# Splitting the later filter loads over two DMA queues, and releasing the weight loads after the last filter group

## The chip, the cores and the metric

The kernel runs on one core of a Trainium2 chip. The metric is the time of one execution on the device, in microseconds (us). Executions are in a fast or a slow state. In the slow state the granted TensorE clock is low (0.655 in one profile below), and such runs are set aside. A "profile" is one traced execution. Times inside a profile count from its first instruction, and its span is 1.5 to 2 us shorter than the time of the execution.

Each DMA is issued by an engine's queue: SyncE (SP), ScalarE (ACT) or GpSimd (POOL). A transfer has "landed" when its completion semaphore, the counter that others wait for, has got its last count. To "evict" is to copy TensorE's results to where the next step reads them.

## The reference, cut to what matters

```python
X = np.fft.rfft(x, axis=1)                     # x: 8 batches x 3008 x 256
y = np.fft.irfft(X * (filt_r + 1j*filt_i), n=3008, axis=1)
h = y.reshape(24064, 256) @ w_in               # 256 -> 2048
out = (h / (1 + exp(-beta*h))) @ w_out         # 2048 -> 256
```

The kernel does the Fourier transforms as small matmuls. Batch 0 is transformed in a set-up of some 38 us. The main loop then multiplies by the weights, and the transforms of the later batches are worked in between its steps.

## The kernel before

In the set-up the filter comes in three groups of columns. GpSimd issues the first, SyncE the other two. Each group is four transfers: a lower and an upper half, of the real and of the imaginary filter. SyncE issues a tiny transfer (`mark`) first. It reads the third piece of the first x, so SyncE's queue is held until that piece has landed.

```python
mark = dpool.tile([1, D], BF16, name="mark", tag="mark")
nc.sync.dma_start(mark[:], x_cur[:1, JG, :])
...
FG = ((0, KG), (KG, KG), (2 * KG, 2 * KG))
for h in range(2):
    for f, at in ((filt_r, 0), (filt_i, M)):
        load_filter(fri, f, at, *FG[0], gp)[h]()
for h in (1, 0):
    for f, at in ((filt_r, 0), (filt_i, M)):
        load_filter(fri, f, at, *FG[1], nc.sync)[h]()
for h in (0, 1):
    for f, at in ((filt_r, 0), (filt_i, M)):
        load_filter(fri, f, at, *FG[2], nc.sync)[h]()
```

VectorE multiplies with the filter: 12 steps of two products. Steps 0 to 2 need the first group, 3 to 5 the second, 6 to 11 the third.

```python
for dst, ps in zip((p_t, q_t), pss):
    nc.vector.tensor_tensor(dst[:], ps[:], fri[:, 2 * i : 2 * i + 2, :], ALU.mult)
```

GpSimd issues the weights and the second x, after a tiny copy (`held`) that waits for filter rows:

```python
for p0 in (H, M + H):
    gp.tensor_copy(held[p0 : p0 + H], fri[p0 : p0 + H, 2 * KG - 1, :1])
load_win(0); load_win(1); load_wout(0)
xs[1] = load_x(1, X_HALVES[:2])
...                                  # at step 3 of the products:
load_wout(1)
load_x(1, X_HALVES[2:], xs[1])
mark3 = dpool.tile([1, D], BF16, name="mark3", tag="mark3")
nc.sync.dma_start(mark3[:], xs[1][:1, J - 1, :])   # holds SyncE's queue until this x is there
load_wout(2); load_wout(3)
...
for at in (0, M):                                  # four loads, next on SyncE's queue
    for go in load_filter(frr, filt_r, at, 0, JG, nc.sync): go()
```

## Time and profile before

| | before |
|---|---|
| time, five fast runs | median 792.15 us (790.61 to 792.77) |
| span of the profile | 788.4 us |
| TensorE busy | 777.5 us (99%) |
| first matmul of the main loop | 38.26 us |

The engine line of the page of the kernel before says what bounds it: TensorE is busy nearly all the time.

```profile
span 788.4 us, 15540 instructions
PE 777.5 (99%) x6111; PEld 547.9 (69%) x6111; DVE 394.4 (50%) x647; ACT 597.4 (76%) x920; POOL 144.6 (18%) x143
```

The next lines are from the timeline of VectorE, kernel before: start, duration, instruction, and in brackets the idle time before it and what the profile takes for the releaser. They are the products of steps 0, 3 and 6, the first users of the three filter groups.

```profile
17.18 0.69 DVE L446 TENSOR_TENSOR pb_t<-ps,fri 128x512 bf16<-128x512 f32 x1 [1.23 <-PE ps L437]
...
21.24 0.68 DVE L446 TENSOR_TENSOR pb_t<-ps,fri 128x512 bf16<-128x512 f32 x1
...
27.01 0.69 DVE L446 TENSOR_TENSOR pb_t<-ps,fri 128x512 bf16<-128x512 f32 x1 [0.64 <-PE ps L437]
```

```profile
51.53 0.59 PE L825 MATMUL hps<-y,win_sb 128*128 128x512 bf16 x2
51.96 0.33 PE L546 MATMUL ps<-t4b,zz 96*128 96x94 bf16 x4
```

### The profile page before, as it was taken

What the parts mean: (1) busy time and instruction counts of PE and PEld (TensorE: products, weight loads), DVE (VectorE), ACT (ScalarE), POOL (GpSimd) and SP (SyncE); (2) the same over time, 40 slices, a digit from 0 to 9 for tenths busy, and PEclk for the clock granted to TensorE, in tenths of its full rate; (3) what the DMA queues carried; (4) which work ended last, traced back from release to release, by engine and by line L of the source; (5) the groups of instructions that cost most, each with busy time, mean ns of one, the idle gap of its engine ahead of it and who ended that gap; (6) DMA issues with size and microseconds to landing.
All of it is one profiled execution on the core that took longest, in us unless ns stands there. A gap on an engine that the chain in (4) does not pass through costs nothing.

```text
span 788.4 us, 15540 instructions
## 1 busy us (share of the span) xinstructions
PE 777.5 (99%) x6111; PEld 547.9 (69%) x6111; DVE 394.4 (50%) x647; ACT 597.4 (76%) x920; POOL 144.6 (18%) x143
## 2 busy tenths in 40 slices
PE   8899999999999999999999999999999999999997
PEld 5766667766777667876668766686667766776665
DVE  7847835646536564465635746267462761500101
ACT  6887886886678866788677876778767788677776
POOL 9422500420014200131002310024000340000000
PEclk9999999999999999999999999999999999999999
DMA  9978687116901187012860238412370214100101
GB/s 193 233 199 214 161 207 206 48 67 187 234 27 67 48 214 206 28 67 94 198 176 27 95 103 186 151 55 85 103 215 29 74 67 127 51 31 28 54 27 54
DMA packets 84057, 91.46 MB, mean 116 GB/s; under 512 B 4434, under 2 KB 74212, under 8 KB 82962
## 3 DMA queue, kind: packets, MB, share of 16 engines
q1 hardware_dynamic: 80880, 73.95, 30.6%
q0 software_dynamic: 2816, 16.26, 10.6%
q8 instruction: 48, 0.79, 0.4%
q10 hardware_dynamic: 288, 0.26, 0.1%
q14 instruction: 25, 0.20, 0.1%
HBM read 57.16 MB, written 46.66 MB: 132 GB/s over the span
## 4 chain that ended last, share of the span: by engine, by line
PE 90%; DMA 5%; DVE 3%; issue 1%; POOL 0%; DVEq 0%; ACT 0%; POOLq 0%; SPq 0%; ACTq 0%
PE acc L860 40%; PE hps L825 39%; PE ps L621 3%; PE ps L546 2%; PE ps L643 2%; PE ps L669 2%; DMA fri<-in_filt_i_dram 1%; DMA d<-a 1%; DVE ost L109 1%; DMA xg<-in_x_dram 1%; DMA mark<-xg 1%; DMA a<-d 0%; DVE qb_t L446 0%; DVE q_t L658 0%; DVE pb_t L446 0%
## 5 line engine op out<-in xcount | busy, mean ns | idle before, releaser
L834 ACT ACTIVATE gT<-hps,beta_sb 128x512 bf16<-128x512 f32 x752 | 516.8, 687 | 175.2 <-PE hps L825 165.5
L860 PE MATMUL acc<-wout_sb,gT 128*128 128x256 bf16 x3008 | 455.1, 272 | 1.2 <-ACT ost L107 0.2
L825 PE MATMUL hps<-y,win_sb 128*128 128x512 bf16 (+8 forms) x1730 | 447.7, 351 | 0.0
L860 PEld LDWEIGHTS <-gT 128*128 128x128 bf16 x3008 | 285.4, 98 | 132.4 <-issue 4.3
L825 PEld LDWEIGHTS <-win_sb 128*128 128x128 bf16 x1730 | 164.9, 98 | 24.3 <-issue 0.2
L659 POOL TENSOR_TENSOR v_t<-p_t,q_t 128x512 bf16<-128x512 f32 x84 | 106.7, 1271 | 374.5 <-DVE q_t L658 371.6
L109 DVE COPY ost<-acc 128x512 f32<-128x512 f32 (+1 forms) x88 | 56.2, 677 | 193.6 <-PE acc L860 190.6
L109 DVE CAST a<-ps 96x512 bf16<-96x512 f32 x96 | 65.8, 686 | 86.1 <-PE ps L621 83.7
L111 DVE TENSOR_SCALAR y<-ps 128x376 bf16<-128x376 f32 (+1 forms) x119 | 64.4, 545 | 63.1 <-PE ps L546 62.9
L654 DVE TENSOR_TENSOR p_t<-ps,frr 128x512 f32<-128x512 f32 x84 | 58.1, 692 | 32.4 <-PE ps L643 29.8
L658 DVE TENSOR_TENSOR q_t<-ps,fri 64x512 f32<-64x512 f32 x84 | 58.3, 694 | 1.2
L655 DVE SCALAR_TENSOR_TENSOR q_t<-ps,fri 64x512 f32<-64x512 f32 x84 | 57.5, 684 | 1.1
L546 PEld LDWEIGHTS <-zz 96*128 96x128 bf16 x512 | 35.3, 97 | 28.9
L107 ACT ACTIVATE z<-ps 128x512 bf16<-128x512 f32 x84 | 49.5, 590 | 0.8 <-PE ps L669 0.7
L621 PE MATMUL ps<-xg,t 94*96 94x512 bf16 x112 | 41.9, 381 | 0.0
L546 PE MATMUL ps<-t,zz 96*128 96x94 bf16 x448 | 36.7, 204 | 0.0
L118 POOL DMA_DIRECT2D xg<-in_x_dram x22 | 12.1, 557 | 114.3 <-PE acc L860 97.7
L669 PE MATMUL ps<-v_t,t 128*128 128x256 bf16 x168 | 32.1, 273 | 0.6 <-DVE q_t L658 0.6
L643 PE MATMUL ps<-a,t 128*128 128x256 bf16 x168 | 32.1, 273 | 0.3 <-DMA a<-d 0.3
L643 PEld LDWEIGHTS <-t 128*128 128x128 bf16 x168 | 15.9, 98 | 15.0 <-issue 0.4
L621 PEld LDWEIGHTS <-t 94*96 94x96 bf16 x112 | 13.8, 123 | 12.1
L669 PEld LDWEIGHTS <-t 128*128 128x128 bf16 x168 | 15.4, 98 | 8.4 <-DVE q_t L658 1.4
(119 smaller groups left out, 195.8 us busy)
## 6 DMA issues: line engine op xcount, KB each, us to landing
out_dram<-ost SPq DMA_DIRECT2D x80, 256.0 KB, 2.1
d<-a SPq DMA_DIRECT2D x28, 384.0 KB, 3.7
a<-d SPq DMA_DIRECT2D x28, 384.0 KB, 5.1
d<-z SPq DMA_DIRECT2D x28, 384.0 KB, 2.3
zz<-d SPq DMA_DIRECT2D x28, 384.0 KB, 6.6
xg<-in_x_dram POOLq DMA_DIRECT2D x6, 1280.0 KB, 10.1
frr<-in_filt_r_dram SPq DMA_DIRECT2D x12, 256.0 KB, 7.5
out_dram<-ost SPq DMA_DIRECT2D x18, 128.0 KB, 3.6
```

The source lines that it names most:

```text
L109: nc.vector.tensor_copy(dst, src)
L111: nc.vector.tensor_scalar_mul(dst, src, scale)
L546: nc.tensor.matmul(ps[:, e, :NP], lhsT=zz[:, jj + e, dc * P : (dc + 1) * P], rhs=tab[:], start=True, stop=True,)
L621: nc.tensor.matmul(ps[:KP], lhsT=t1[:], rhs=s["x"][:, 2 * i : 2 * i + 2, :], start=True, stop=True)
L643: nc.tensor.matmul(ps[:, e, :], lhsT=t2[:, k0 + e, 3:5, :].rearrange("p c k -> p (c k)"), rhs=s["a2"][g][:, kk + e, :], start=True, stop=True,
L654: nc.vector.tensor_tensor(p_t[:], ps[:], frr[:, ks_, :], ALU.mult)
L658: nc.vector.tensor_tensor(q_t[:M], ps[M:P], fri[M:P, ks_, :], ALU.mult)
L659: nc.gpsimd.tensor_tensor(v_t[:], p_t[:], q_t[:], ALU.add)
L669: nc.tensor.matmul(ps[:, e, :], lhsT=t3[:, k0 + e, :], rhs=v_t[:, e, :], start=True, stop=True)
L825: nc.tensor.matmul(hps[:, pos - t0 : pos - t0 + ln], lhsT=win_sb[:, dc, fb * P : (fb + 1) * P], rhs=ys[b][:, dc, n0 : n0 + ln], start=(dc ...
L834: nc.scalar.activation(gT[:, :tn], hps[:, :tn], ACT.Silu, scale=beta_sb[:, fb : fb + 1])
L860: nc.tensor.matmul(acc[tb // per][:, tb % per, :], lhsT=gT[:, tb * P : (tb + 1) * P], rhs=wout_sb[:, fb, :], start=(fb == 0 and tb % per = ...
```

## The change

The intent: load the real and the imaginary filter side by side on two queues, and keep the weights out of their way by releasing them only when the last group's rows are there.

```diff
-    for h in (1, 0):
-        for f, at in ((filt_r, 0), (filt_i, M)):
-            load_filter(fri, f, at, *FG[1], nc.sync)[h]()
-    for h in (0, 1):
-        for f, at in ((filt_r, 0), (filt_i, M)):
-            load_filter(fri, f, at, *FG[2], nc.sync)[h]()
+    def load_later(f, at, eng):
+        for part, order in ((1, (1, 0)), (2, (0, 1))):
+            for h in order:
+                load_filter(fri, f, at, *FG[part], eng)[h]()
+
+    load_later(filt_r, 0, nc.sync)
...
     for part in (1, 2):
         t2_part(0, part)
+    load_later(filt_i, M, nc.scalar)
...
-    for p0 in (H, M + H):
-        gp.tensor_copy(held[p0 : p0 + H], fri[p0 : p0 + H, 2 * KG - 1, :1])
+    for p0 in (0, M):
+        gp.tensor_copy(held[p0 : p0 + H], fri[p0 : p0 + H, NK - 1, :1])
```

## The prediction

> What bounds the kernel now. The engine summary gives TensorE 777.5 of 788.4 us (99%), at full granted clock in every slice. From 38 us on the main loop's matmuls run back to back, so a shift at its start reaches the end. Only the set-up can gain, and there the timeline of VectorE decides: its first product (pb_t) starts at 17.18 us and the 24 products with a few copies run to 35.2 us; the one gap, 0.64 us, is put down to a matmul.
>
> Do the products wait for filter rows? The first started 0.8 us after its matmul; what came last was the first filter group, issued by GpSimd (landed 17.0 us), which the change leaves alone. The second group is first used at 21.24 us (one of its transfers landed at 17.9), the third at 27.01 us. The chain of waits shows "fri<-in_filt_i" ending at 25.17 us, but VectorE was then at work: no idle time hangs on it. Quicker second and third groups gain about 0.
>
> Do weights compete? Hardly. GpSimd issues the first at 18.72 us, but its packets start after 23 us, when SyncE's queue has nearly drained; from 3 to 42 us the DMA engines are full. The Trainium skill ("DMA: Bandwidth & Descriptors", Queues, rings and completion order) says that each engine alternates between queues by packets; this trace looks more like order of issue: filter transfers issued on SyncE from 9.6 us start moving at about 13 us. The same page (Issuing engines are not separate DMA queues) says that a second issuing engine saves only issue time: here 0.47 us a transfer on SyncE, which is idle anyway.
>
> What the change adds. Four issues enter ScalarE's stream after its last table activation (ends 11.59 us). ScalarE is next needed at 12.82 us, for five evictions of the first stage (2.03 us). Four issues at 0.47 us would delay them 0.6 us. Worse, eight DMA semaphores are reused in turn by both queues: in the trace SyncE's tenth transfer waited 1.5 us, until 14.30, for the tiny "mark" transfer. In the new order the tenth is ScalarE's fourth. So ScalarE should evict from 14.7 instead of 12.8: 1.9 us late. The transposes of a_t then start near 16.8 instead of 14.86, the first product near 18.4 instead of 17.18, and, ScalarE being full from 17 to 27 us, about 1.4 us should reach the end of the set-up.
>
> Later weights: held should end at 23 to 24 us instead of 18.7, a DMA bubble of about 1 us. Slack: the first half of the second x landed at 36.2, needed at 39.1; its second half at 41.7, needed at 46; weight scalings end about 5 us ahead of use. Cost about 0, at most 1 us.
>
> Sum: 0 gained, 1.4 us lost in the set-up, 0 to 0.5 us for late x or weights, loop unchanged. From 792.8 I predict 794.2 us, 80% range 791.5 to 797.0. Chances: faster by over 2% 0.01, within 2% 0.97, slower by over 2% 0.02.
>
> Right if: ScalarE issues four transfers from about 11.5 us, the last after 14 us, released by mark; evicts a_t from 14.7; first product at 18.2 to 18.6; first hps matmul 1.4 us after 38.27; weights issued at 23 to 24 us. Wrong if: the fourth issue does not wait (then +0.5 us); the imaginary second group lands after 22.4 us (VectorE idles before the fourth product); the second x stalls the loop near 40 or 47 us (several us); or the first group lands earlier, as fewer of SyncE's bytes run beside it (up to 1 us gained).

## More of the kernel before

In the first steps of the loop, the first-stage rows of batch 1 are evicted into buffers `a1` and written out to DRAM (`d<-a`) by SyncE. There are four such groups and three buffers, of which one is used for `zz0` first. The fourth group therefore has to wait until the first write has left its buffer.

```python
apool = pool("apool", 3)
zz0[0] = apool.tile([KP, JG, D], BF16, name="zz", tag="a1")
...
if jj == 0:
    s["a1"] = apool.tile([KP, JG, D], BF16, name="a1", tag="a1")
...
evac(s["a1"][:, jj : jj + 2, :], ps[:KP], on_act)
if jj + 2 == JG:
    nc.sync.dma_start(s["d1r"][:, g * JG : (g + 1) * JG, :], s["a1"][:])
```

SyncE's queue in the kernel before (timeline): the first mark, the tenth transfer of the hardware queues, the second mark, and the first d<-a write (four merged into one line).

```profile
9.33 0.27 SPq L198 DMA_DIRECT2D mark<-xg  x1
...
14.32 0.32 SPq L134 DMA_DIRECT2D fri<-in_filt_i_dram  x1
...
41.10 0.24 SPq L507 DMA_DIRECT2D mark<-xg  x1
...
43.23 10.86 SPq L626 DMA_DIRECT2D d<-a  x4
```

GpSimd's queue (timeline) shows the release of the weights, and TensorE's timeline shows no bracket, hence no idle time, near 52 us:

```profile
18.36 0.42 POOL L409 COPY held<-fri 32x1 f32<-32x1 f32 x2
18.72 1.54 POOL L412 DMA_DIRECT2D win_sb<-in_moe_w_in_dram  x2
```

## The result, and the profile after

The changed kernel took 793.12 us (median of 6 fast runs, 791.62 to 794.11), the kernel before 792.23 us (median of all its 6 runs, among them the slow one of 1008.37). The ratio is 1.0016, 95% interval 0.9998 to 1.0033. Ratios here are the mean time of one kernel's fast runs over that of the other's of the same rounds, so not quite the ratio of these medians. A later comparison of the kernel before with itself gave 1.0018 (0.9994 to 1.0042), so 0.16% is no more than the noise of this method. What happened has to be read from the profiles.

The engine line of the page of the changed kernel (some matmul records are missing from this trace: 6015 of 6111, so its busy time is not to be compared):

```profile
span 790.3 us, 15444 instructions
PE 772.3 (98%) x6015; PEld 548.2 (69%) x6111; DVE 394.2 (50%) x647; ACT 597.3 (76%) x920; POOL 144.9 (18%) x143
```

VectorE's timeline, changed kernel, the same three products:

```profile
17.01 0.69 DVE L447 TENSOR_TENSOR pb_t<-ps,fri 128x512 bf16<-128x512 f32 x1 [0.47 <-PE ps L438]
...
22.34 0.69 DVE L447 TENSOR_TENSOR pb_t<-ps,fri 128x512 bf16<-128x512 f32 x1 [1.19 <-DMA fri<-in_filt_i_dram]
...
27.06 0.68 DVE L447 TENSOR_TENSOR pb_t<-ps,fri 128x512 bf16<-128x512 f32 x1
```

The wait at step 6 is gone, and a new one stands at step 3, where the second group of the imaginary filter comes 1.19 us late. The set-up as a whole is as long as before: the first matmul of the loop starts at 38.30 us (38.26 before; in three later profiles with the old set-up it started at 38.53 to 39.68 us).

ScalarE's timeline, changed kernel: its four issues and the next eviction.

```profile
10.48 0.41 ACTq L134 DMA_DIRECT2D fri<-in_filt_i_dram  x1
...
11.89 0.43 ACTq L134 DMA_DIRECT2D fri<-in_filt_i_dram  x1
12.48 1.65 ACT L107 ACTIVATE a_t<-psa 128x384 bf16<-128x384 f32 x4 [0.89 <-PE psa L327]
```

The fourth issue did not wait, though only just: by the semaphore events `mark` had landed at 11.84 us. And ScalarE evicts even a little earlier than before (12.82 us). The step on which the prediction rested did not take place in this execution.

The loss is in the loop. GpSimd's queue, then SyncE's, then TensorE near 52 us, each from the timeline of the changed kernel:

```profile
24.07 0.41 POOL L410 COPY held<-fri 32x1 f32<-32x1 f32 x1 [5.09 <-DMA fri<-in_filt_i_dram]
24.54 1.54 POOL L413 DMA_DIRECT2D win_sb<-in_moe_w_in_dram  x2
```

```profile
7.60 0.27 SPq L198 DMA_DIRECT2D mark<-xg  x1
...
43.85 0.23 SPq L508 DMA_DIRECT2D mark<-xg  x1
...
45.96 9.60 SPq L627 DMA_DIRECT2D d<-a  x4
```

```profile
51.78 0.38 PE L826 MATMUL hps<-y,win_sb 128*128 128x512 bf16 x1
53.91 0.33 PE L547 MATMUL ps<-t4b,zz 96*128 96x94 bf16 x4 [1.75 <-DVE a L109]
```

TensorE idles 1.75 us. It waits for VectorE (`a`), and the list of waits from 44 to 60 us says what VectorE waited for (time in total, how often, longest). First the kernel before, then the changed one:

```profile
DVE a L109 <- DMA d<-a: 2.3, 1, 2.3
```

```profile
DVE a L109 <- DMA d<-a: 4.8, 1, 4.8
...
PE ps L547 <- DVE a L109: 1.7, 1, 1.7
```

The start of that delay shows in the view of stretches: start and end, length, busy time of each engine, clock, DMA share and, last, GB/s. Before, then after:

```profile
25.00:26.00 1.00, 0.95 (x15) 0.75 (x13) 1.00 (x3) 0.87 (x3) 0.00 (x0) 1.00 1.16 219
```

```profile
24.00:25.00 1.00, 1.00 (x18) 0.98 (x16) 0.97 (x5) 0.56 (x1) 0.86 (x2) 1.00 0.05 16
25.00:26.00 1.00, 1.00 (x18) 0.98 (x16) 1.00 (x3) 1.00 (x3) 1.00 (x2) 1.00 0.00 0
```

In the changed kernel the DMA engines stand idle for about two microseconds, between the last filter rows and the first weights. All loads behind come that much later. Thus the second mark, which waits for the second x, is issued at 43.85 instead of 41.10 us (+2.75), the first d<-a write at 45.96 instead of 43.23, and it lands at 53.04 instead of 50.54. VectorE's fourth group of rows needs the buffer that this write reads.

### The profile page after: what moved, and what is told of

The parts are those of the page before. It is cut to its first block, busy times and chain, and to the rows that moved or that the text cites. A ratio compares the mean times of both kernels' runs of the same rounds, so it can differ in the third digit from the quotient of the medians.

```text
span 790.3 us, 15444 instructions
## 1 busy us (share of the span) xinstructions
PE 772.3 (98%) x6015; PEld 548.2 (69%) x6111; DVE 394.2 (50%) x647; ACT 597.3 (76%) x920; POOL 144.9 (18%) x143
## 4 chain that ended last, share of the span: by engine, by line
PE 88%; DMA 6%; DVE 2%; issue 2%; ACT 1%; POOL 1%; SPq 0%; DVEq 0%; ACTq 0%; POOLq 0%
PE acc L861 41%; PE hps L826 36%; PE ps L622 3%; PE ps L547 3%; PE ps L644 2%; DMA d<-a 2%; PE ps L670 2%; DMA xg<-in_x_dram 2%; DMA fri<-in_filt_i_dram 2%; DVE ost L109 1%; PE pw L187 1%; DMA a<-d 0%; DVE q_t L659 0%; DVE q_t L656 0%; DVE p_t L655 0%
## 5 line engine op out<-in xcount | busy, mean ns | idle before, releaser
L826 PE MATMUL hps<-y,win_sb 128*128 128x512 bf16 (+8 forms) x1636 | 427.4, 350 | 0.1
```

The costliest lines, as they stand in the source:

```text
L826: nc.tensor.matmul(hps[:, pos - t0 : pos - t0 + ln], lhsT=win_sb[:, dc, fb * P : (fb + 1) * P], rhs=ys[b][:, dc, n0 : n0 + ln], start=(dc ...
```

## The experiments

Theory 1: the late release is what costs, by the path second x, SyncE's second mark, d<-a write, buffer. Theory 2, that of the prediction: ScalarE's issues cost, by their wait for `mark`. Twelve runs were made, three of them repeats of a kernel: the first four on one chip, the second four on another and the last four on a third, each group beside runs of the kernel before. "PE idle" is TensorE's idle time before the matmul named, from its timeline.

### 1. The two queues without the late release (split_only)

```diff
-    for p0 in (0, M):
-        gp.tensor_copy(held[p0 : p0 + H], fri[p0 : p0 + H, NK - 1, :1])
+    for p0 in (H, M + H):
+        gp.tensor_copy(held[p0 : p0 + H], fri[p0 : p0 + H, 2 * KG - 1, :1])
```

> The changed kernel with the old release of the weights: the real and imaginary filter on two queues, but the weights wait only for the second group's rows, as before. Theory 1 (the late release costs): the second x lands near 41 to 42 us again, the first d<-a write is issued near 43 us, TensorE has no idle time over 0.3 us between 50 and 55 us (1.75 us in the changed kernel), and the time is that of before: ratio to before 0.999 to 1.001. Theory 2, the rival of the prediction (the four issues on ScalarE cost): the first matmul of the main loop comes about 1.4 us later than before's 38.27 us, ratio about 1.0015 to 1.002, and TensorE's idle time at 50 to 55 us plays no part.

Measured: ratio 0.9992 (0.9978 to 1.0006). No idle time near 52 us. So far theory 1. But this profile also showed what the prediction had said and the first profile had not. Here x came later, and mark was issued at 9.65 us instead of 7.60. ScalarE's timeline:

```profile
11.41 0.44 ACTq L131 DMA_DIRECT2D fri<-in_filt_i_dram  x1
15.30 0.33 ACTq L134 DMA_DIRECT2D fri<-in_filt_i_dram  x1
15.67 1.64 ACT L107 ACTIVATE a_t<-psa 128x384 bf16<-128x384 f32 x4 [4.08 <-PE pt L354]
```

The bracket names a matmul, but the instruction in front is the fourth issue, and by the semaphore events of this trace `mark` had landed at 15.28 us. The first product came at 19.27 us and the loop at 40.41 us, 2.15 us late. The profiled run was also the slowest of its five (792.08; the others 790.04 to 790.98). Both theories describe something real; the second depends on when x lands.

There is a third thing in this profile. From 19.14 to 22.56 us the granted clock of TensorE was 0.5, and the 2.15 us contain what that cost. The view of stretches shows it (the clock is the third number from the end):

```profile
20.00:21.00 1.00, 1.00 (x8) 0.75 (x6) 0.84 (x2) 0.71 (x1) 0.17 (x1) 0.50 1.13 265
```

### 2. The late release without the two queues (gate_only)

The kernel before with only the last hunk of the change.

> The kernel before with the late release alone: all later filter groups on SyncE's queue, weights wait for the third group's rows. Theory 1: weights issued near 23 us or later, second x lands near 43 to 44 us, the first d<-a write is issued near 45 to 46 us and lands near 53 us, TensorE idles 1 to 2 us near 52 us; ratio to before about 1.0015 to 1.0025. Theory 2: same as before, ratio 0.999 to 1.001, no idle time near 52 us.

Measured: ratio 1.0025 (1.0009 to 1.0041), as theory 1 says. On the same chip and in the same rounds this kernel's mean is 793.91 us and split_only's 790.91. TensorE's timeline shows two waits, one directly for x (39 to 40 us) and the one for the buffer:

```profile
39.97 0.63 PE L621 MATMUL ps<-xg,t 94*96 94x512 bf16 x2 [1.10 <-DMA xg<-in_x_dram]
...
55.38 0.33 PE L546 MATMUL ps<-t4b,zz 96*128 96x94 bf16 x4 [2.46 <-DVE a L109]
```

The two waits sum to 3.56 us, but the mean time rose by 2.4 us against before. This profile does not stand for the mean: its run was the slowest of the six (796.02 us; the others 791.94 to 795.11), and its span is 5.8 us longer than that of before. It also has a wait of 0.96 us at 138 us, and after the stall at 55.38 us TensorE's granted clock was 0.5 from 55.58 to 58.99 us:

```profile
56.00:57.00 1.00, 1.00 (x6) 0.66 (x5) 0.31 (x1) 0.76 (x2) 0.00 (x0) 0.50 0.05 15
```

Half of these 3.4 us, 1.7 us, is an estimate of what the slow clock cost. With it the sum comes out: 3.56 + 0.96 + 1.7 us, less the 0.43 us by which the loop started earlier (37.83 us), are 5.8 us. Five of the six runs of gate_only show a mean clock of 0.998 or less, one of the 11 runs of before beside it. So part of the 2.4 us is clock: by the mean clocks, 0.9977 against 0.9995 over some 790 us, about 1.4 us, an estimate. The drop begins 0.2 us after the stall ends, but stalls of 1.75 and 2.32 us in the changed kernel were followed by none, and no run here tests what causes it.

### 3. A buffer of its own for the fourth group (after_a1_free, a1_free_again)

```diff
-            s["a1"] = apool.tile([KP, JG, D], BF16, name="a1", tag="a1")
+            own = b == 1 and g == NJG - 1
+            s["a1"] = (zzpool if own else apool).tile(
+                [KP, JG, D], BF16, name="a1", tag="zz" if own else "a1"
+            )
```

> The changed kernel, with a buffer of its own for the last group of first-stage rows of the second batch (taken from a pool that has one free then), so that this eviction need not wait for the first d<-a write. Theory 1 in its full form (the lateness of x reaches TensorE only through that buffer): x still lands near 44 us and d<-a near 53 us, but VectorE's wait on d<-a (4.8 us) and TensorE's idle 1.75 us near 52 us are gone; ratio to before 0.999 to 1.001. If the lateness reaches TensorE by another way (x itself, weights, the later a<-d read), the idle time stays or reappears within the first 70 us and the ratio stays near 1.002. Theory 2: ratio stays near 1.002, lost before 38 us.

The first time, the profile is of no use; the five fast runs gave 0.9987 (0.9973 to 1.0001), a little below the expected range. So it ran again:

> The changed kernel with the buffer of its own once more, as its profile fell in the slow state. Theory of the late x through the buffer: second mark near 44 us, first d<-a write landed near 53 us or later, yet no TensorE idle over 0.3 us at 50 to 56 us; ratio to before 0.998 to 1.000. Otherwise an idle time over 1 us stays there.

Measured: ratio 1.0008 (0.9992 to 1.0025), so the time repeats badly and misses the range. But the profile is clear. The second mark came at 44.14 us and the first d<-a write landed at 53.43 us, as late as in the changed kernel, and TensorE did not stop:

```profile
51.34 0.60 PE L864 MATMUL acc<-wout_sb,gT 128*128 128x256 bf16 x4
51.78 0.59 PE L829 MATMUL hps<-y,win_sb 128*128 128x512 bf16 x2
52.21 0.33 PE L547 MATMUL ps<-t4b,zz 96*128 96x94 bf16 x4
```

So in the changed kernel the late x reached TensorE through that buffer. (This profile had 1.28 us of another idle time, near 133 us; see experiment 8.)

### 4. The d<-a writes ahead of the second mark (after_d_first)

```diff
-                mark3 = dpool.tile([1, D], BF16, name="mark3", tag="mark3")
-                nc.sync.dma_start(mark3[:], xs[1][:1, J - 1, :])
...
-    for at in (0, M):
-        for go in load_filter(frr, filt_r, at, 0, JG, nc.sync):
-            go()
...
-            for k0 in range(JG, NK, JG)
+            for k0 in range(0, NK, JG)
```

> The changed kernel without the second mark transfer, which makes SyncE's queue wait for the second x, and with the four first loads of the other copy of the filter moved behind the a<-d reads. So the d<-a writes may be issued as soon as their rows are evicted. Theory 1: first d<-a write issued near 43 to 44 us though x lands near 44, landed by about 51 us or earlier, no TensorE idle over 0.3 us near 52 us; ratio to before 0.999 to 1.001. If instead the late x or the late weights themselves hold TensorE, ratio stays near 1.002. A new wait is possible: the filter's copy must land before about 66 us, where VectorE first multiplies with it.

Measured: ratio 1.0046 (1.0031 to 1.006), worse than all others. The idle time near 52 us is gone, as expected, and the first write landed at 49.05 us. But it was issued at 45.99 us, not at the expected 43 to 44 and no earlier than in the changed kernel (45.96); it landed sooner because it took 3.06 us instead of 7.08. And other costs are in this profile. ScalarE's fourth issue waited again, until 15.57 us, and the loop started at 41.25 us. From 17.36 to 24.19 and from 75.39 to 78.80 us the granted clock was 0.5. And the possible new wait that the expectation had named came: the moved filter rows were late for the products of batch 1 (VectorE's timeline).

```profile
72.61 0.69 DVE L649 TENSOR_TENSOR p_t<-ps,frr 128x512 f32<-128x512 f32 x1 [4.69 <-DMA frr<-in_filt_r_dram]
```

So it fits the path but does not prove it: as the loop started 2.95 us later, even a write that landed at 53.04 us would have been in time by the rule of experiment 7. And it is no remedy.

### 5. The changed kernel again (after_again)

> The changed kernel itself once more, for a second profile and six more times. In the first profile ScalarE's fourth filter issue did not wait (mark had been issued at 7.60 us, and was done before 11.89 us); in two other kernels with the same code on ScalarE mark was issued at 9.65 and 9.95 us and the fourth issue waited until 15.30 and 15.57 us. Theory: an execution goes one way or the other with the landing of the third piece of the first x (near 7.6 or near 9.6 us). If this profile has mark issued near 9.6 us, the fourth issue waits until about 15.3 us, the first hps matmul comes 2 to 3 us later than 38.3 us, and the late-x stall near 52 us shrinks or is gone. If mark is issued near 7.6 us, the profile repeats the first. Ratio to before 1.0015 to 1.003 either way.

Measured: ratio 1.0013 (0.9991 to 1.0035; expected 1.0015 to 1.003), span 792.3 us. Mark was issued at 7.71 us and the fourth issue at 12.14 us, so again no long wait. The loop started at 38.52 us, and TensorE idled 2.32 us near 54 us and another 1.36 us at 136 us. So both profiles of the changed kernel lost in the loop and not in the set-up.

### 6. No reuse of the semaphore of mark (after_no_reuse, split_no_reuse)

The framework gives the transfers of both hardware queues eight completion semaphores in turn. In the trace `mark` and ScalarE's fourth issue carry the same semaphore. With one transfer fewer they no longer do:

```diff
-    load_later(filt_r, 0, nc.sync)
+    for k0, n, h in ((KG, KG, 1), (KG, 3 * KG, 0), (2 * KG, 2 * KG, 1)):
+        load_filter(fri, filt_r, 0, k0, n, nc.sync)[h]()
```

With the late release:

> The changed kernel with the real filter's two lower-half loads of SyncE's queue made one transfer of 18 columns: nine transfers on the two hardware queues before the loop instead of ten, so none of ScalarE's reuses the semaphore of mark. Predicted mechanism right: ScalarE's fourth issue never waits, whatever the time of mark; ScalarE evicts a_t from about 12.5 us; the first hps matmul comes at 37.8 to 38.6 us. The stall by the late x near 52 us (1.5 to 2.5 us) stays, so the ratio to before stays near 1.002. If the set-up is late even so, the reuse is not the cause.

and with the early one:

> As the last, with the weights released early as in the kernel before: neither the wait on mark nor the late x. Both causes right: first hps matmul at 37.8 to 38.6 us, no TensorE idle near 52 us, ratio to before 0.997 to 1.000. If a part of the cost lies in the issue from ScalarE or in the two queues as such, ratio 1.001 or more.

Measured: 1.0014 (0.9995 to 1.0033) with the late release, 0.9989 (0.9971 to 1.0008) with the early one. The fourth issue came at 11.89 us in both, although in split_no_reuse mark was issued at 9.65 us and landed at 15.35 us, just as in split_only, where ScalarE stood until 15.30. The loop started at 37.67 us here and at 40.41 us there: in this pair of profiles the reuse costs 2.7 us, the stretch at half the clock in split_only included. The edit also merges two transfers, but that is not what counts in this pair: in split_only VectorE waited for no later filter rows (step 3 started 2.6 us after theirs had landed). (The first-loop matmul of after_no_reuse at 37.04 us is earlier than the expected 37.8.)

One expectation failed: split_no_reuse still had 1.60 us of PE idle near 53 us. The "early" release came only at 20.5 us, as the imaginary second group, now behind the real filter, landed late (its first half at 20.42 us). But that is not the cause: in split_only the release came at 20.8 us and in before at 18.6 us, and in all three the first load of the weights (`load_win(0)`) landed at 28.1 to 28.2 us. What differs is the landing of the second x that the second mark reads: 42.98 us here and 40.06 us in split_only. Each of these transfers raises its semaphore 16 times in the trace; here 13 of the 16 counts were there by 39.75 us, and the last three came 1.1 to 3.2 us later. Why these parts were late stays open.

The two kernels differ in the release alone and ran in the same rounds: mean 793.11 (792.0 to 794.36) against 791.16 us (790.03 to 792.17), six runs each. The difference is 1.95 us, with a 95% interval of about plus or minus 1.0 us worked out from these twelve times.

### 7. The kernel before with a later x (before_x_late)

```diff
                 load_wout(1)
+                load_wout(2)
+                load_wout(3)
                 load_x(1, X_HALVES[2:], xs[1])
                 ...
-                load_wout(2)
-                load_wout(3)
```

> The kernel before with one order changed: the second half of the second x is loaded after the last two parts of the output weights instead of before them, so it lands about 4.5 us later (near 46 us instead of 41.7) with filters, queues and release as before. If lateness of x is what costs in the changed kernel, with nothing else of it needed: second mark issued near 45.5 us, first d<-a write lands near 54 to 55 us, TensorE idles 2.5 to 4 us at 50 to 56 us, set-up unchanged (first hps matmul near 38.3 us), ratio to before 1.003 to 1.005. If it costs nothing (ratio 0.999 to 1.001), the theory of the late x falls.

Measured: ratio 1.0009 (0.9985 to 1.0033). The second mark came at 44.87 us (expected 45.5) but the d<-a write landed at 52.86 us (not 54 to 55), as it took only 5.86 us, probably because fewer weights were in its way. PE idle was 1.01 us, not the expected 2.5 to 4. The ratio lies in the range (0.999 to 1.001) that was to make the theory of the late x fall. It does not decide that, as its interval holds no loss as well as the 1.01 us seen (0.13%); but by time this experiment did not support the theory. The idle time does fit the path. Here are the fast profiles of all kernels that share the buffer; the last column is the landing of the first d<-a write minus the loop's start minus 13.0 us, and for the two marked with a star also minus the 1.1 us that TensorE had waited for x before:

| kernel | loop starts | second mark | first d<-a landed | PE idle near 52 to 55 us | landed − start − 13.0 |
|---|---|---|---|---|---|
| before | 38.26 | 41.10 | 50.54 | 0 | −0.7 |
| before_again | 39.68 | 42.47 | 52.17 | 0 | −0.5 |
| after_d_first | 41.25 | none | 49.05 | 0 | −5.2 |
| split_only | 40.41 | 40.08 | 49.35 | 0 | −4.1 |
| before_x_late | 38.85 | 44.87 | 52.86 | 1.01 | 1.0 |
| split_no_reuse | 37.67 | 42.99 | 52.28 | 1.60 | 1.6 |
| after | 38.30 | 43.85 | 53.04 | 1.75 | 1.7 |
| after_no_reuse* | 37.04 | 44.12 | 53.36 | 2.13 | 2.2 |
| after_again | 38.52 | 44.38 | 53.84 | 2.32 | 2.3 |
| gate_only* | 37.83 | 44.90 | 54.52 | 2.46 | 2.6 |

The rule fits with one constant, chosen from these rows: the loop can run 13.0 us before it needs that buffer back. Everything beyond is idle time, microsecond for microsecond. The two profiles with the late write and a buffer of their own (a1_free_again, and split_best of experiment 8) would idle 1.9 and 1.8 us by this rule, and idle 0 there. The kernel before had 0.5 to 0.7 us to spare.

### 8. The kernel before again, and two kernels without the costs found (before_again, split_best, before_best)

> The kernel before against itself, for a second profile and for the noise of the comparison. Ratio 0.999 to 1.001. In the profile, the spread of other profiles should be seen here too: mark issued anywhere from 7.6 to 9.7 us, SyncE's tenth issue waiting for it, and TensorE's wait for the second a<-d read near 132 us between 0 and 1.4 us (0.26 us in the first profile); no TensorE idle near 52 us.

Measured: ratio 1.0018 (0.9994 to 1.0042) for the kernel against itself, outside the expected 0.999 to 1.001: the noise is larger than was thought. The profile (span 791.1) held the most useful line, the product of step 6 in VectorE's timeline:

```profile
28.42 0.69 DVE L446 TENSOR_TENSOR pb_t<-ps,fri 128x512 bf16<-128x512 f32 x1 [2.30 <-PE ps L437]
```

This is the wait of 0.64 us in the first profile, now 2.30 us long, and the loop starts at 39.68 us. The matmul named had long been done (ended at 25.22 us by the profile). The semaphore events in the traces tell the releaser: the last transfer of the third filter group, at 28.25 us. The same for other kernels, with the last landing of the second and third groups, and VectorE's idle time before the product that uses them first:

| kernel | third group landed | step 6 starts, idle | second group landed | step 3 starts, idle |
|---|---|---|---|---|
| before | 26.83 | 27.01, 0.64 | 19.56 | 21.24, 0 |
| before_again | 28.25 | 28.42, 2.30 | 20.01 | 21.14, 0 |
| before_x_late | 27.42 | 27.59, 2.23 | 19.03 | 20.57, 0 |
| gate_only | 26.40 | 26.58, 0.19 | 21.48 | 21.60, 0.22 |
| after | 25.16 | 27.06, 0 | 22.22 | 22.34, 1.19 |
| after_again | 25.34 | 27.28, 0 | 22.44 | 22.56, 1.41 |
| split_no_reuse | 26.33 | 26.41, 0 | 21.38 | 21.70, 0 |

So the kernel before did wait for filter rows, and the change removes that wait: its gain. In gate_only and before_again the last filter transfer was issued within 0.1 us of the same time (15.06 and 15.16 us), and landed at 26.40 and 28.25 us. With the weights held back it came 1.85 us earlier in this pair; against the other three profiles with the old loads and the early release (26.83 to 27.42 us) it came 0.4 to 1.0 us earlier. The Trainium skill, "DMA: Bandwidth & Descriptors", section "Queues, rings and completion order", says that an engine takes turns between the queues that have work. These landings fit that: weights released early would run beside the last filter transfer and stretch it. But it is one profile against four that differ among themselves by 1.4 us, so it is likely and not shown. At the other end, SyncE's filter loads were issued from 9.6 us and their data moved from about 13 us, which looks as if one queue waits for the backlog of another; no run here separates the two.

The same profile had 1.52 us of PE idle at 135 us for the second a<-d read (these reads bring the rows of the d<-a writes back). In the first profile of before it was 0.26 us, in after 0, in after_again 1.36. There, GpSimd's load of the next x runs ahead of the last d<-a write of batch 2 (issued at 118.02 us in before, landed 10.30 us later). So the last two kernels have the buffer of their own, and load each later x 18 steps later; split_best also has the edit of experiment 6 and the early release.

```diff
-            place(a - 8, a - 8, ux(b + 1), per=9)
+            place(a + 10, a + 10, ux(b + 1), per=9)
```

> The two queues with all costs found taken away: no reuse of the semaphore of mark on ScalarE, weights released early, the buffer of its own, and the load of each later x placed 18 steps later, so that it no longer runs just ahead of the d<-a write of the batch before (10.3 us to landing near 118 us in before, 3 us where nothing is in its way) and the a<-d read near 132 us no longer holds TensorE. Expected: no TensorE idle over 0.4 us after 38 us; ratio to before 0.996 to 0.999. If the two queues as such gain or lose something, this differs from the next run by over 1 us.

> The kernel before, its filter loads and its release untouched, with the buffer of its own and the later load of x alone. Expected: no TensorE idle over 0.4 us after 38 us; ratio to before 0.997 to 1.000, and within 1 us of the run with two queues, as the filter rows were in time before the change.

Measured: split_best 789.46 us, ratio 0.9984 (0.9968 to 0.9999); before_best 790.03 us, ratio 0.9986 (0.9972 to 0.9999). In both profiles TensorE has no idle time over 0.40 us after 38 us. (The d<-a write landed after 3.50 us in split_best.) The two differ by 0.16 us in their means, which is nothing: with the other costs gone, two queues are worth no more than one, as far as these times can tell. (In the profiles the loop starts at 37.03 us with two queues and at 38.53 us with one, 1.50 us earlier; the spans differ by 1.3 us. A gain of that size is not excluded, as six runs each leave more than 1 us of doubt.) Both look quicker than before by 1.2 to 1.4 us in the mean, but the kernel against itself differed by 1.4 us in the same rounds. A gain is likely from the idle times that vanished, and not proven by time.

## Why the prediction was right or wrong

The number was right, 794.2 us predicted with a range of 791.5 to 797.0, and 793.12 measured. This was luck: the way to it was largely wrong, errors cancelled, and the range holds the kernel before too (792.15 us).

- "Quicker second and third groups gain about 0": wrong. Step 6 of the products waited for the third group, 0.64 us in the very profile that the prediction read, and 2.13 to 2.30 us in three others with the old loads and release (before_again, before_x_late, before_best). The prediction took the profile's releaser (a matmul) at its word.
- "Do weights compete? Hardly": probably wrong. In the one profile of the old loads with the weights held back, the last filter transfer landed 0.4 to 1.85 us earlier than in the four others.
- "The imaginary second group lands after 22.4 us" was listed as a way to be wrong, and nearly so it was: 22.22 and 22.44 us, with 1.19 and 1.41 us of idle time. That is more than the 0.64 us gained at the third group against the first profile, and over half of the 2.13 to 2.30 us against the others.
- ScalarE's fourth issue waiting for mark, "1.4 us lost in the set-up": the mechanism is real, but it hangs on chance. It did not occur in the two profiles of the changed kernel (the loop began 0.04 and 0.26 us later than in before's first profile, and no later than in the other three with the old set-up). Of the four other profiles with the same issue code it occurred in three: split_only, after_d_first and a1_free_again, where the issue waited until 15.30, 15.57 and 14.51 us (the fourth is slow). Removing the reuse removed it (experiment 6). In a1_free_again the first product came at 18.48 us, as predicted for that case, and yet the loop started only at 38.51 us, as by then all later filter rows were in time (step 3 started 1.5 us after their landing, step 6 1.9 us after it). So even there 1.4 us was too much for that profile, and too little for split_only (2.15). One difference shows: during the set-up the granted clock was 0.5 for 3.4 us in split_only and for 6.8 us in after_d_first (loop at 41.25 us), and never in a1_free_again. The prediction did not reckon with the clock.
- "A DMA bubble of about 1 us": about 2 us, and the second x came 2.75 us later. "Cost about 0, at most 1 us": 1.75 and 2.32 us. This term was mis-sized because the slack was read at TensorE's own use of x, and not along SyncE's queue: mark, four filter loads, d<-a write, buffer, with 0.5 to 0.7 us to spare.
- The sum: predicted loss 1.4 + 0 to 0.5; found in the first profile 0.04 + 1.75, of a span 1.9 us longer. So its loss stood in the wrong place: the set-up, where 1.4 us were expected, lost nothing, and the loop, said to be unchanged, lost all of it.

What stays open: why the third piece of the first x lands anywhere from 7.6 to 9.9 us, which decides when mark is issued; how often the unprofiled runs of the changed kernel had the wait on ScalarE; what halves the granted clock in some executions; why parts of the second x are late in split_no_reuse; and why one merged transfer on SyncE let the imaginary second group land at 20.72 instead of 22.22 us.

## What to carry to other kernels

When loads are released later, follow every queue that stands behind them to its last consumer, buffers included: the slack is that of the tightest link, not that of the first reader. Before you move DMA issues onto a busy engine, look at which earlier transfer's completion semaphore each will reuse: here ScalarE stood still until that transfer had landed (15.30 us in split_only). And where the profile names a releaser that had finished long before, look up when the operands' transfers landed; here it turned "nothing to gain" into a wait of up to 2.3 us. Last, look at the granted clock stretch by stretch: a mean of 0.997 hid 3.4 us at 0.5.

## What the Trainium skill lacked or had wrong

- "DMA: Bandwidth & Descriptors", section "Issuing engines are not separate DMA queues", says that issuing from several engines only saves the issuing time of a sequencer. The times agree, within over 1 us of doubt, that two queues gave no more than one (0.9984 against 0.9986), but the section does not say that a transfer moved to a compute engine can stop that engine: the reuse of a completion semaphore held ScalarE's stream until 15.30 us, and the loop started 2.7 us later than in its counterpart without the reuse (3.4 us at half the granted clock included).
- The same page's section "Rules for kernel authors" asks for a semaphore dedicated to the DMA; it does not say what eight semaphores taken in turn cost when a slow small transfer is among them. It has no figure for a small transfer behind a backlog: mark, 0.5 KB, landed 4.97 us after its issue in before and 5.6 us in split_only, while others were loading.
- "Why a DMA increments its semaphore by 16 and not by 1" on that page says that a transfer on few engines raises its semaphore at once by the rest and later by the landing. Nothing is lacking here; the traces agree: mark's semaphore had two events, 9.75 us (0.42 after its issue) and 14.30 us.
- "Perfetto Trace Analysis", section "DMA Instruction — HWDGE (DVE, Sync)", says that the profile's record of such an instruction covers the issue alone and not the movement of the data. The traces agree: the line of mark is 0.27 us long, and it landed 4.97 us after its start. The section does not say that issues on ScalarE can run beside the activations ahead of them. Here they did: in the changed kernel the first was issued at 10.48 us, while the table activations ran until 11.59 us, and each issue took 0.41 to 0.45 us. The prediction counted them from 11.59 us.
